# Statistics by tile, W1 in three loads, sixteen filler products and a new order in a fused attention and MLP kernel

## The chip, the cores and the metric

The kernel runs on one core of a Trainium2 chip. A core has five engines that run side by side: TensorE (PE, matrix products, with its weight loads shown as PEld), VectorE (DVE), ScalarE (ACT), GpSimd (POOL) and SyncE (SP, which here only issues DMA transfers). The metric is the device time of one execution in microseconds (us); lower is better.

## The reference

The input x has 2048 tokens of width 448. It is normalized, goes through a linear attention with 16 heads of 28 and through an MLP with 1792 hidden units, and both results are added to x:

```python
xn = _layernorm(x, axis=-1)
return x + _A_ref(xn, A_wqkv, A_w_phi, A_wo) + _B_ref(xn, B_w1, B_b1, B_w2)

def _A_ref(x, wqkv, w_phi, wo):
    ...
    pq = jnp.einsum("bhsd,hdf->bhsf", q, w_phi)
    pk = jnp.einsum("bhsd,hdf->bhsf", k, w_phi)
    phi_q = jnp.concatenate([_softmax(pq, axis=-1), _softmax(-pq, axis=-1)], axis=-1)
    phi_k = jnp.concatenate([_softmax(pk, axis=-1), _softmax(-pk, axis=-1)], axis=-1)
    kv = jnp.einsum("bhsf,bhsd->bhfd", phi_k, v)
    z  = jnp.einsum("bhsf->bhf", phi_k)
    num = jnp.einsum("bhqf,bhfd->bhqd", phi_q, kv)
    den = jnp.einsum("bhqf,bhf->bhq", phi_q, z)[..., None] + 1e-6
    ...

def _B_ref(x, w1, b1, w2):
    h = jnp.einsum("bsd,df->bsf", x, w1) + b1
    sp = jnp.log1p(jnp.exp(-jnp.abs(h))) + jnp.where(h > 0, h, jnp.zeros_like(h))
    act = h * jnp.tanh(sp)
    return jnp.einsum("bsf,fd->bsd", act, w2)
```

## The kernel before

The tokens are cut into 16 tiles t of 128; two tiles make a pair u (0 to 7). The kernel is a list of small steps, each named by a short word. The string ORDER is a list of these words, written out by hand or by a planner outside the kernel: the steps are called in that order, and each puts its instructions at the end of the queues of the engines that it uses. Each engine works through its own queue strictly in that order. What a step reads and writes is declared, and waits are derived from it; a wait holds up everything behind it on the same engine.

The steps, by their words:

- `lx0` to `lx6` load x (tiles 0-1, 2-3, 4-5, 6-7, 8-11, 12-15), `lkm`, `lvm`, `lkt` the weights of k and v (`lkt` their last 64 rows, in two transfers), `lp` w_phi, `lb` the bias b1, `l1m` and `l1t` W1 (rows 0 to 383 in one transfer, L271, and the last 64 rows twice, L276), `lo` and `l2` Wo and W2. A last letter s or a says whether SP or ScalarE issues it. `lqT0` to `lqT3` load Wq by a transposing DMA (L280); `qd` copies a part of it (L284).
- `st` makes the mean and variance of a tile or pair, on VectorE (two instructions, L456 and L458) or on ScalarE (L447 to L452), `rs` the reciprocal root (ScalarE L470 and L472, or POOL L464 and L467), `xn` the normalized pair (VectorE L491; with letter p on POOL, L486, after a small `shift` on VectorE). `xt` transposes it: letter m by a DMA from SP (L511), which also waits until tiles 0 and 15 of x have landed; else by TensorE (L499) with a copy out of PSUM (L504, L506).
- `z` is a run of filler products (L371) on TensorE; nothing reads their result. `wtk`, `wmk`, `wmq` fold w_phi into the weights of k and q (products L551 and L575), giving Wpk and Wpq; `b1` transposes the bias.
- `v`, `k`, `q` of a pair and `f0.c`, `f1.c` (the first MLP product for chunk c of the hidden units and half of the tokens) come in two parts: F, six products over 128 rows, and H, two products over 64 rows that run side by side in the two halves of the array (L426). The first part of the two takes a pair of PSUM banks; after the second the result is taken out: v by ScalarE or VectorE (L504, L506), k and q by two Exp (L613, L674) and f by one Mish (L693) on ScalarE. There are four pairs of banks; a new key takes the pair unused for longest, and waits for whoever empties it.
- `kn` normalizes half of a pair's k (VectorE L621 and L623, then POOL L625); `kv` sums k times v over all tokens (L642), one step per pair, and `kvz` masks the result and transposes it by DMA. `e` transposes a tile of q by DMA (L682). The q of three pairs shares three buffers, so a later Exp waits for an earlier `e`.
- `nd` forms numerator and denominator of a tile (L716, and eight VectorE instructions from L731 to L742), `ot` transposes the result by DMA (L750), `wo` (parts F and H, L832) and `g` (L816) make the output of a pair or tile, and `fin` adds x to it on VectorE (L781). `sto` and `stt` store a pair or tile; the last word of ORDER names the tile that is finished last, whose last 64 columns are done apart (L795 to L802) and whose store is split over ScalarE's and SP's queue (L843).

SP's queue holds nearly all loads, all transposes and all stores, in the order of ORDER. In the profile all of SP's transfers are on one queue (q1) and ScalarE's on another (q10).

## Time and profile before

| what | value |
|---|---|
| time, median of 3 runs | 153.97 us (153.91 to 154.64) |
| profiled execution: its span from first to last instruction | 152.5 us (its page gives no other time for it) |
| TensorE busy | 147.9 us, 97% |
| VectorE busy | 101.2 us, 66%; ScalarE 74.9 us, 49%; POOL 39.9 us, 26% |
| transfers | 39961 packets, 17.17 MB |
| engines in the first 50 us | VectorE and ScalarE are busy nine tenths and more in most slices |

The profile page names groups of instructions by line, engine and tiles ("out<-in"), gives their count, busy time and the mean length of one in ns, and the idle time of the engine before them with what ended it. The chain is followed back from the last instruction through whatever released each step. In the timeline each row has its start and length in us. TensorE's products overlap: one 379 ns long starts while the one before is still draining, so the distance of starts, not the length, is what a product costs.

### The profile page before, as it was taken

The numbers are of one execution on the slowest core, as the hardware profiler recorded it, in microseconds if no ns is written. First come the engines' busy times: TensorE is split into PE (matmuls) and PEld (weight loads), VectorE is DVE, ScalarE is ACT, GpSimd is POOL, SyncE is SP. The second block draws the span as 40 slices with busy tenths as digits, with TensorE's granted clock in tenths as the row PEclk, the third lists the DMA queues.
The fourth block names the chain that finished last, engine by engine and source line by source line (L and its number), as shares of the span: only waits on it lengthen the run. The fifth ranks groups of instructions, "written<-read, shape, count | busy, mean of one in ns | idle before, by whom it ended". The sixth has DMA issues, their size and how long they took to land.

```text
span 152.5 us, 2888 instructions
## 1 busy us (share of the span) xinstructions
PE 147.9 (97%) x1181; PEld 72.7 (48%) x1181; DVE 101.2 (66%) x227; ACT 74.9 (49%) x91; POOL 39.9 (26%) x58
## 2 busy tenths in 40 slices
PE   7899999999998999999999999999999999999993
PEld 2365444454443466444444444555555555455552
DVE  1699997999999203198999847798695970311221
ACT  4888899898599996757459657100000000000000
POOL 7452552499999950000000000000000000000000
PEclk9999999999999999999999999999999999999999
DMA  5995576889969176830379941030206111110302
GB/s 130 274 238 97 175 136 127 177 236 257 189 141 192 24 160 55 135 71 0 64 149 302 338 75 25 4 62 6 54 0 195 50 34 26 60 34 0 120 0 90
DMA packets 39961, 17.17 MB, mean 113 GB/s; under 512 B 33932, under 2 KB 39180, under 8 KB 39948
## 3 DMA queue, kind: packets, MB, share of 16 engines
q1 hardware_dynamic: 39804, 16.89, 49.2%
q8 instruction: 9, 0.15, 0.4%
q10 hardware_dynamic: 144, 0.10, 0.2%
q14 instruction: 4, 0.03, 0.1%
HBM read 7.02 MB, written 1.84 MB: 58 GB/s over the span
## 4 chain that ended last, share of the span: by engine, by line
PE 82%; DMA 7%; ACT 6%; SPq 2%; DVE 0%; issue 0%; ACTq 0%
PE PS L426 40%; PE PS L816 28%; PE PS L832 7%; DMA EqT<-actT 4%; DMA Wkv<-in_A_wqkv_dram 3%; PE PS L716 3%; PE PS L642 2%; ACT actT L613 2%; ACT actT L693 1%; ACT actT L674 1%; PE PS L575 1%; ACT L693 1%; ACT v_all L504 1%; SPq L268 1%; SPq L682 1%; PE PS L551 0%
## 5 line engine op out<-in xcount | busy, mean ns | idle before, releaser
L426 PE MATMUL PS<-xnT,W 128*128 128x512 bf16 (+1 forms) x224 | 46.3, 379 | 0.0
L816 PE MATMUL PS<-W,actT 128*128 128x448 bf16 (+1 forms) x224 | 42.8, 351 | 0.0
L693 ACT ACTIVATE actT<-PS,b1T 128x1024 bf16<-128x1024 f32 x28 | 30.3, 1114 | 13.1 <-PE PS L426 13.0
L816 PEld LDWEIGHTS PS<-W,actT 128*128 128x128 bf16 x224 | 21.8, 98 | 20.2 <-issue 0.4
L426 PEld LDWEIGHTS PS<-xnT,W 128*128 128x128 bf16 (+1 forms) x224 | 17.6, 97 | 23.7 <-issue 5.1
L625 POOL TENSOR_TENSOR actT<-actT,rSk 128x896 bf16<-128x896 bf16 x16 | 26.6, 1701 | 4.4 <-DVE rSk L623 4.4
L781 DVE TENSOR_TENSOR x_all<-PS,x_all 128x448 bf16<-128x448 f32 (+1 forms) x16 | 9.6, 617 | 20.9 <-PE PS L816 17.7
L621 DVE TENSOR_REDUCE Sk<-actT 128x32 f32<-128x896 bf16 x16 | 16.7, 1042 | 0.9 <-ACT actT L613 0.9
L613 ACT ACTIVATE actT<-PS 128x896 bf16<-128x896 f32 x16 | 13.7, 940 | 0.4 <-PE PS L426 0.4
L426 PE MATMUL PS<-Wpq,xnT 128*128 128x448 bf16 (+1 forms) x64 | 12.9, 353 | 0.5 <-ACT actT L693 0.5
L426 PE MATMUL PS<-Wpk,xnT 128*128 128x448 bf16 (+1 forms) x64 | 12.7, 353 | 0.0
L426 PE MATMUL PS<-Wkv,xnT 128*128 128x448 bf16 (+1 forms) x64 | 12.6, 353 | 0.0
L731 DVE COPY Sq<-PS 128x16 f32<-128x16 f32 x32 | 4.0, 167 | 10.8 <-PE PS L716 10.8
L456 DVE BATCH_NORM_STATS2 stats<-x_all 128x6 f32<-128x448 bf16 x14 | 8.5, 605 | 3.4 <-DMA x_all<-in_A_x_dram 3.4
L739 DVE TENSOR_TENSOR v_all<-v_all 128x464 f32<-128x464 f32 x16 | 10.3, 642 | 0.6
L735 DVE TENSOR_TENSOR v_all<-PS,Sq 128x464 f32<-128x464 f32 x16 | 10.3, 641 | 0.5
L742 DVE TENSOR_TENSOR xn<-v_all,rden 128x448 bf16<-128x448 f32 x16 | 10.0, 625 | 0.6
L737 DVE TENSOR_TENSOR v_all<-PS,Sq 128x464 f32<-128x464 f32 x16 | 10.1, 629 | 0.0
L674 ACT ACTIVATE actT<-PS 128x896 bf16<-128x896 f32 x10 | 8.5, 932 | 1.7 <-DMA EqT<-actT 1.7
L426 PEld LDWEIGHTS PS<-Wpq,xnT 128*128 128x128 bf16 (+1 forms) x64 | 5.3, 97 | 6.5 <-issue 1.1
L426 PEld LDWEIGHTS PS<-Wpk,xnT 128*128 128x128 bf16 (+1 forms) x64 | 5.3, 97 | 6.1 <-issue 1.9
L426 PEld LDWEIGHTS PS<-Wkv,xnT 128*128 128x128 bf16 (+1 forms) x64 | 5.0, 97 | 5.7 <-issue 1.5
(86 smaller groups left out, 118.0 us busy)
## 6 DMA issues: line engine op xcount, KB each, us to landing
W<-in_B_w_dram SPq DMA_DIRECT2D x1, 1568.0 KB, 7.8
out_dram<-x_all SPq DMA_DIRECT2D x7, 224.0 KB, 2.2
W<-in_B_w_dram SPq DMA_DIRECT2D x1, 1344.0 KB, 9.0
x_all<-in_A_x_dram SPq DMA_DIRECT2D x4, 224.0 KB, 3.2
x_all<-in_A_x_dram SPq DMA_DIRECT2D x2, 448.0 KB, 4.6
Wkv<-in_A_wqkv_dram SPq DMA_DIRECT2D x2, 336.0 KB, 4.5
Wo<-in_A_wo_dram SPq DMA_DIRECT2D x2, 336.0 KB, 3.9
W<-in_B_w_dram SPq DMA_DIRECT2D x2, 224.0 KB, 3.6
```

The costliest lines, as they stand in the source:

```text
L426: ins = e.matmul(o, lhs(c, k), rhs(c, k), start=first and c in (0, 3), stop=not first and c in (2, 3))
L613: op("ACT", lambda e, s=s: e.activation(E_of(u)[:, s, :, :], two(b, D), ACT.Exp, scale=1.0 if s == 0 else -1.0), r=[pb(b), pb(b + 1)], w=[ ...
L621: op("DVE", lambda e: e.tensor_reduce(Sk[u][:, s, :], Eh(), AX.X, ALU.add), r=[("E", u, s)], w=[("Sk", u, s)], tag=f"Sk{u}.{s}")
L625: op("POOL", lambda e: e.tensor_tensor(Eh(), Eh(), ap_on(rSk[u][:, s, 0:1], [[1, 2 * H], [0, DH]]), ALU.mult), r=[("E", u, s), ("rSk", u, ...
L674: op("ACT", lambda e, s=s: e.activation(Eq_of(u)[:, :, s, :].rearrange("p i (h n) -> p i h n", n=64)[:, :, :, 0:QP], two(b, D).rearrange(" ...
L693: op("ACT", lambda e: e.activation(actT[:, fc, q * 1024:(q + 1) * 1024], bank(b, 2), ACT.Mish, bias=b1T[:, fc:fc + 1]), r=[("b1T",), pb(b) ...
L735: op("DVE", lambda e: e.tensor_tensor(tv(t1[i]), num(0), sx(1), ALU.mult), r=[pb(b), pb(b + 1), ("Sq", i, 1)], w=[("t1", i)], tag=f"ta{t}")
L737: op("DVE", lambda e: e.tensor_tensor(tv(t2), num(1), sx(0), ALU.mult), r=[pb(b), pb(b + 1), ("Sq", i, 0)], w=[("t2",)], tag=f"tb{t}")
L739: op("DVE", lambda e: e.tensor_tensor(t1[i], t1[i], t2, ALU.add), r=[("t1", i), ("t2",)], w=[("t1", i)], tag=f"tc{t}")
L742: op("DVE", lambda e: e.tensor_tensor(o_sb[(t // 2) % 2][:, t % 2, :].rearrange("p (h d) -> p h d", d=DH), t1[i][:, :, 0:DH], ap_on(rden[i ...
L816: ins = e.matmul(bank(b)[:, 0:width(t)], actT[:, fc, tok(t)], W2[:, fc, 0:width(t)], start=first and fc == 0, stop=last and fc == FC - 1)
L832: ins = e.matmul(bank(b)[:, 0:n], oT_of(u)[lo:hi, cc * P:(cc + 1) * P], Wo[lo:hi, cc, 0:n], start=first and c in (0, 3), stop=last and c i ...
```

## The change

The products stay the same but for four more fillers. What changes is:

- `st` and the statistics go by tile: `st6d` is tile 6 on VectorE, `st2a` tile 2 on ScalarE (before, a pair at a time, with letter b one tile on each). `rs` gets a letter t: logarithm and root for each of the two tiles by itself on ScalarE. A tile's xn waits for its own root only.
- rows 0 to 383 of W1 come in three transfers, `l1m0` to `l1m2`, each a word of its own.
- the fillers read a constant 1.0 that the framework writes at the start; the tile of zeros and its memset are gone, and there are 16 instead of 12 (`z16`).
- which step first waits for the old contents of an ot buffer follows the order (`homes_taken`) instead of being the even pair.
- ORDER is new throughout. Pairs 3 and 1 are transposed on TensorE instead of 2 and 3; pairs 6 and 7 are normalized on POOL instead of 5; ScalarE makes the statistics of tiles 2 and 5 instead of 5 and 7; w_phi is loaded by ScalarE's queue; b1 is loaded and transposed much later; Wo and W2 are loaded earlier.

```diff
@@ -145,18 +145,19 @@
 
 
 ORDER = """
-table lx2s zero lx3s pv st2b pw lkms lps pi pm st3b rs3a lkts z12 pp lbs rs2p lx1s xn2d xn3d wtk0b xt2b wtk1b lvms
-lx4s lqT2 st1 bd pk lqT0 xt3a b1 wmk0b lqT1 rs1a wmk1a xn1d st5 rs5p v2Fd lqT3 v3Fa v3Ha k2H v2Ha k3H qd xt1m lx0s
-st4 k2F rs4p wmq0d xn4d xn5p wmq1a k3F v1Fd st0 q3F k1H q3H lx6s st6 v1Hd q2H q2F rs6p st7 k1F q1F rs0p xt4m xt5m
-xn6d k4F rs7p k4H e6 v5Hd xn0d xt6m xn7d kn4.1 q1H k5H xt0m v5Fd k5F kn5.0 v6Fd kn5.1 k6F k0H xt7m ep e7 v6Ha k7H
-l1ts l1ms k6H k7F kn6.0 k0F kn6.1 e3 q6F e2 v0Fa kn2.1 kn7.1 v4Fd v0Ha v4Hd kn4.0 q6H v7Hd kn3.0 v7Fa q4F e4 e12
-f1.2H q4H e9 f0.2H kn2.0 e13 f0.2F kn7.0 f0.0F f1.2F f0.1F f0.0H f0.1H f1.3H q5H kn1.0 f1.3F kn0.1 e8 q0F q0H f0.3H
-kn0.0 q7H kn3.1 e5 e1 q5F q7F f0.3F f1.7F kv7 kn1.1 kv0 kv4 kv6 kv3 kv2 kv1 e0 kv5 e10 f1.1H kvz f1.7H f1.8H f1.1F
-f1.8F f0.6F e14 e11 f1.5H f0.6H nd2 f0.10F f1.5F nd1 f0.10H f0.5H f0.5F f1.11F nd3 ot1m f1.11H nd0 f0.13H f0.13F e15
-f1.12F f1.0F f1.0H ot0m f1.12H los wob nd6 f1.13F f0.7F f1.10H f0.7H nd7 l2s ot3m f1.13H f1.10F f0.4F f0.4H nd5
-f0.12H f0.9H f0.9F f0.12F nd4 f0.11H f0.8H f0.8F f0.11F f1.4F f1.6H f1.4H nd10 ot2m f1.9H f1.9F f1.6F wo3F wo3H nd11
-nd13 nd12 ot5m ot6m g7 g6 g10 g11 wo5H nd15 nd14 wo2H wo5F ot7m g5 sto3 g4 wo2F wo6F sto5 wo6H wo1H nd9 nd8 wo1F sto2
-g12 g2 g14 g13 wo7F wo0F ot4m wo0H sto6 wo4H wo7H g3 g0 wo4F g1 g8 stt14 sto0 g9 sto1 sto4 g15 stt15
+lpa lx1s pi lx3s lkms lkts lvms table lx2s st3d pp pw pm lqT1 st6d st2a pv st7d z16 rs3t rs1a xn3d xn1d lqT2 lqT3 lqT0
+wtk0b bd xt3b wtk1b xt1d wmk0b st4d v3Fd wmk1d st5a lx6s qd rs2t xn2d lx0s v1Fd v1Ha v3Ha st15d st14d rs7p k1F wmq1d
+st12d xn7p wmq0a lx4s st10d xt2m k3F st9d st8d rs4p st11d rs5p st13d k1H l1ts k3H xn4d xt7m q3H q1H q1F l1m2s rs6p q3F
+xn5d xn6p q2F k2F kn3.0 xt4m v2Fd v2Hd xt5m q2H st0d st1d k2H xt6m v7Ha v7Fa rs0p k7F k4F k7H l1m1s e3 xn0d k4H xt0m
+v5Hd k6H lbs pk kn1.1 kn3.1 k6F v5Fd kn7.0 kn6.1 k5F k0F k5H e6 kn5.0 v6Ha q4H kn2.0 e2 k0H q4F l1m0s e7 v6Fd ep q6F
+v0Fd b1 v0Hd q6H f1.3H f0.0H f1.3F e8 f1.1F f0.0F kn5.1 kn7.1 kn0.1 v4Fa e9 v4Ha kn1.0 f1.0H e13 e12 f1.1H f0.1H kn4.1
+kn4.0 f1.0F f0.1F f1.2F los q7H kn6.0 q5H kn0.0 f1.2H q0H e5 e4 kn2.1 q7F q5F q0F f1.13F kv5 kv0 kv7 kv4 kv3 kv6 kv1
+kv2 f0.13H f1.13H f0.12H f0.12F f0.13F e0 kvz wob f0.3F e1 f1.8H f0.3H f0.11H l2s nd0 f1.8F f0.11F f1.10F nd1 f1.10H
+ot0m e10 e14 e11 f1.9H nd2 f1.9F f1.12F f0.8F f1.12H f0.7H f0.8H nd3 f0.7F f0.2F f1.7F nd5 e15 f1.7H f1.11H f0.2H
+f1.11F f0.9F nd4 f1.4H f0.10H f0.9H f1.4F f0.10F ot1m ot2m f0.6F f0.4H f0.5H f0.6H nd12 f0.5F f0.4F f1.5F nd13 f1.6H
+ot6m nd8 f1.5H f1.6F g0 g1 wo6F nd7 wo0H nd9 wo6H g12 g13 ot4m wo2F wo0F g5 wo2H nd6 ot3m nd10 nd11 g4 g8 g7 g9 wo3H
+ot5m nd15 nd14 wo4H ot7m g6 wo4F g14 g2 g3 g11 wo1F wo7F wo5F wo1H wo5H wo7H sto1 wo3F g10 sto6 sto0 sto5 sto3 sto4
+g15 stt14 sto2 stt15
 """
...
-    zeros = sb("zeros", [P, 2], BF16)
     junk = [sb(f"junk{i}", [P, D], BF16) for i in range(2)]
...
+    def load_chunk(eng, name, dst, src, c):
+        dma(eng, lambda e: e.dma_start(dst[:, c, :], src[c * P:(c + 1) * P, :]), w=[(name, 0, c)], tag=f"ld{name}.{c}")
+
...
     def rows_of(name):
-        return [(name, 0), ("Wt", 0), ("Wt", 1)] if name in ("Wk", "Wv") else [(name, i) for i in range(3)]
+        if name in ("Wk", "Wv"):
+            return [(name, 0), ("Wt", 0), ("Wt", 1)]
+        return [("W1", 0, c) for c in range(3)] + [("W1", 1), ("W1", 2)]
...
     def warm(n):
         b = take1()
+        one = nc.const_aps.tensor(1.0, (P, 1), BF16)
 
         def f(e):
             for _ in range(n):
-                ins = e.matmul(bank(b)[:, :], ap_on(zeros[:, 0:1], [[0, P]]), ap_on(zeros[:, 0:1], [[0, TCW]]), start=True,
-                               stop=True)
+                ins = e.matmul(bank(b)[:, :], ap_on(one, [[0, P]]), ap_on(one, [[0, TCW]]), start=True, stop=True)
             return ins
-        pe(f, [("zeros",)], [pb(b)], f"warm{n}")
+        pe(f, [], [pb(b)], f"warm{n}")
...
-    def ln_stats(u, both=False):
-        for t in (2 * u, 2 * u + 1):
-            if both and t % 2:
-                i = u % 2
-                op("ACT", lambda e, t=t: e.activation(junk[i][:], x_all[:, t, :], ACT.Copy, scale=1.0 / D,
-                                                      accum_out=mv[:, t, 0:1]),
-                   r=[("x", t), ("junk", i)], w=[("mean", t), ("junk", i)], tag=f"sm{t}")
-                op("ACT", lambda e, t=t: e.mul(rmean[:, i:i + 1], mv[:, t, 0:1], D ** -0.5), r=[("mean", t)],
-                   w=[("rmean", i)], tag=f"rm{t}")
-                op("ACT", lambda e, t=t: e.activation(junk[i][:], x_all[:, t, :], ACT.Square, bias=rmean[:, i:i + 1],
-                                                      scale=-D ** -0.5, accum_out=mv[:, t, 1:2]),
-                   r=[("x", t), ("rmean", i), ("junk", i)], w=[("mv", t), ("junk", i)], tag=f"sq{t}")
-                continue
-            op("DVE", lambda e, t=t: e.bn_stats(stats[:, t, :], x_all[:, t, :]), r=[("x", t)], w=[("st", t)],
-               tag=f"bn{t}")
-            op("DVE", lambda e, t=t: e.bn_aggr(mv[:, t, :], stats[:, t, :]), r=[("st", t)], w=[("mv", t), ("mean", t)],
-               tag=f"ag{t}")
+    def ln_stats(t, eng):
+        if eng == "ACT":
+            i = t // 2 % 2
+            op("ACT", lambda e: e.activation(junk[i][:], x_all[:, t, :], ACT.Copy, scale=1.0 / D, accum_out=mv[:, t, 0:1]),
+               r=[("x", t), ("junk", i)], w=[("mean", t), ("junk", i)], tag=f"sm{t}")
+            op("ACT", lambda e: e.mul(rmean[:, i:i + 1], mv[:, t, 0:1], D ** -0.5), r=[("mean", t)], w=[("rmean", i)],
+               tag=f"rm{t}")
+            op("ACT", lambda e: e.activation(junk[i][:], x_all[:, t, :], ACT.Square, bias=rmean[:, i:i + 1],
+                                             scale=-D ** -0.5, accum_out=mv[:, t, 1:2]),
+               r=[("x", t), ("rmean", i), ("junk", i)], w=[("mv", t), ("junk", i)], tag=f"sq{t}")
+            return
+        op("DVE", lambda e: e.bn_stats(stats[:, t, :], x_all[:, t, :]), r=[("x", t)], w=[("st", t)], tag=f"bn{t}")
+        op("DVE", lambda e: e.bn_aggr(mv[:, t, :], stats[:, t, :]), r=[("st", t)], w=[("mv", t), ("mean", t)], tag=f"ag{t}")
...
-               r=[("mv", a), ("mv", a + 1)], w=[("lnv", u)], tag=f"vare{u}")
+               r=[("mv", a), ("mv", a + 1)], w=[("lnv", a), ("lnv", a + 1)], tag=f"vare{u}")
             op("POOL", lambda e: e.tensor_tensor(rstd[:, a:b], lnv[:, a:b], mhalf[:], ALU.pow),
-               r=[("lnv", u), ("eps",)], w=[("rstd", u)], tag=f"rstd{u}")
+               r=[("lnv", a), ("lnv", a + 1), ("eps",)], w=[("rstd", a), ("rstd", a + 1)], tag=f"rstd{u}")
             return
-        op("ACT", lambda e: e.activation(lnv[:, a:b], mv[:, a:b, 1], ACT.Ln, bias=eps_col[:]),
-           r=[("eps",), ("table",), ("mv", a), ("mv", a + 1)], w=[("lnv", u)], tag=f"ln{u}")
-        op("ACT", lambda e: e.activation(rstd[:, a:b], lnv[:, a:b], ACT.Exp, scale=-0.5),
-           r=[("lnv", u)], w=[("rstd", u)], tag=f"rstd{u}")
+        for n, m in ((a, b),) if eng == "ACT" else ((a, a + 1), (a + 1, b)):
+            op("ACT", lambda e, n=n, m=m: e.activation(lnv[:, n:m], mv[:, n:m, 1], ACT.Ln, bias=eps_col[:]),
+               r=[("eps",), ("table",)] + [("mv", t) for t in range(n, m)], w=[("lnv", t) for t in range(n, m)], tag=f"ln{n}")
+            op("ACT", lambda e, n=n, m=m: e.activation(rstd[:, n:m], lnv[:, n:m], ACT.Exp, scale=-0.5),
+               r=[("lnv", t) for t in range(n, m)], w=[("rstd", t) for t in range(n, m)], tag=f"rstd{n}")
...
-        home = [("oT", u)] + ([x for n in oT_home[u // 2][2] for x in home_rows[n]] if u % 2 == 0 else [])
+        home = [("oT", u)] + ([x for n in oT_home[u // 2][2] for x in home_rows[n]] if u // 2 not in homes_taken else [])
+        homes_taken.add(u // 2)
...
-        add(f"st{u}", ln_stats, u)
-        add(f"st{u}b", ln_stats, u, True)
+        for t in (2 * u, 2 * u + 1):
+            for eng, c in (("DVE", "d"), ("ACT", "a")):
+                add(f"st{t}{c}", ln_stats, t, eng)
         add(f"xt{u}b", xT, u, "both")
-        for eng, c in (("ACT", "a"), ("POOL", "p")):
+        for eng, c in (("ACT", "a"), ("POOL", "p"), ("tiles", "t")):
             add(f"rs{u}{c}", ln_rstd, u, eng)
...
-        add(f"l1m{c}", load_main, eng, "W1", W1, B_w1)
+        for i in range(3):
+            add(f"l1m{i}{c}", load_chunk, eng, "W1", W1, B_w1, i)
...
-    for n in (1, 2, 4, 8, 12):
+    for n in (4, 8, 10, 12, 14, 16, 18, 20):
         add(f"z{n}", warm, n)
```

More of the change, by code (lines that the diff above doesn't have):

```diff
@@ L239, in _kernel @@
                  "Wp1": [("Wp", 1, h, c) for h in range(2) for c in range(2)]}
+    homes_taken = set()
     def oT_of(u):
@@ L309, in table @@
            tag="table")
-    def p_zero():
-        op("POOL", lambda e: e.memset(zeros[:], 0.0), w=[("zeros",)], tag="zeros")
     def p_ident():
@@ L480, in ln_pair @@
                                                        ALU.mult),
-               r=[("mean", a), ("mean", a + 1), ("rstd", u)], w=[("sh", u)], tag=f"sh{u}")
+               r=[("mean", a), ("mean", a + 1), ("rstd", a), ("rstd", a + 1)], w=[("sh", u)], tag=f"sh{u}")
         for t in (a, a + 1):
@@ L488, in ln_pair @@
                         op0=ALU.mult, op1=ALU.add),
[L489 removed]
+                       r=[("x", t), ("sh", u), ("rstd", t)], w=[("xn", u % NXN, t % 2, n)], tag=f"xn{t}.{n}")
                 else:
```

5 lines of the change are left out of this document (2 added, 3 removed).

## The prediction

> **What bounds the kernel now.** I read the busy shares first, then the chain that ended last, then the timeline of single engines where the chain leaves TensorE.
>
> ```profile
> span 152.5 us, 2888 instructions
> PE 147.9 (97%) x1181; PEld 72.7 (48%) x1181; DVE 101.2 (66%) x227; ACT 74.9 (49%) x91; POOL 39.9 (26%) x58
> ...
> 7.97 0.65 PE PS L551 x8
> ...
> 15.19 15.00 PE PS L426 x86
> ...
> 35.20 6.42 DMA EqT<-actT
> ...
> 46.90 8.57 PE PS L426 x44
> 55.47 3.27 PE PS L642 x128
> ...
> 119.29 10.59 PE PS L816 x56
> ...
> 149.53 0.56 DVE x_all L781
> ```
>
> TensorE is the bound: from 7.97 to 149.5 the chain is nearly all PE. 56 products of 448 columns take 10.59 us, 0.189 each, so the last two thirds have no room. A new order can gain only in four places: the start (before 7.97), the places where PE waits, the cost of changing from one kind of product to the other, and the end (after 149.5). Where the chain leaves PE (31 to 47 us) PE waits twice:
>
> ```profile
> 38.27 1.30 PE L426 MATMUL PS<-Wpq,xnT 128*128 128x448 bf16 x6
> 39.60 0.39 PE L426 MATMUL PS<-xnT,W 64*128 64x512 bf16 x2
> ...
> 46.90 0.36 PE L426 MATMUL PS<-Wpq,xnT 64*128 64x448 bf16 x2 [0.46 <-ACT actT L693]
> ...
> 30.47 0.59 SPq L271 DMA_DIRECT2D W<-in_B_w_dram  x1
> 31.10 9.71 SPq L682 DMA_TRANSPOSE EqT<-actT  x3
> ...
> W<-in_B_w_dram SPq DMA_DIRECT2D x1, 1344.0 KB, 9.0
> EqT<-actT SPq DMA_TRANSPOSE x10, 3.3
> ...
> 41.69 1.73 ACT L674 ACTIVATE actT<-PS 128x896 bf16<-128x896 f32 x2 [1.67 <-DMA EqT<-actT]
> ```
>
> W1 in one load, issued at 30.47, lands 9.0 us later, at 39.5: the first product on it starts at 39.60, about 0.1 late (the sixth at 0.189 from 38.27 starts at 39.22, plus 0.285 as below). The three transposes queued behind that load take 9.71 us to issue; one lands at 41.6 (35.20 + 6.42), ScalarE waits 1.67 us for its buffer, and PE pays 0.46 at 46.90, with the product's tail (379 ns long, issued every 216) 0.6.
>
> **The start.** Loads lead to the first weight transposes.
>
> ```profile
> 0.95 5.30 PE L371 MATMUL PS<-zeros 128*128 128x512 bf16 x12 [0.95 <-POOL zeros L314]
> 2.71 1.20 SPq L276 DMA_DIRECT2D Wkv<-in_A_wqkv_dram  x2
> 6.02 5.11 SPq L280 DMA_TRANSPOSE WqT<-in_A_wqkv_dram  x4
> ...
> 6.70 0.63 PE L551 MATMUL PS<-ident,Wkv 128*112 128x128 bf16 x8 [0.45 <-DMA Wkv<-in_A_wqkv_dram]
> 7.97 0.65 PE L551 MATMUL PS<-ident,Wkv 128*112 128x128 bf16 x8 [0.23 <-DMA Wkv<-in_A_wqkv_dram]
> ...
> 13.70 1.07 SPq L268 DMA_DIRECT2D x_all<-in_A_x_dram  x2
> ...
> x_all<-in_A_x_dram SPq DMA_DIRECT2D x2, 448.0 KB, 4.6
> ```
>
> Twelve fillers take 5.30 us, 0.44 each, and end at 6.25; at the pace of the later products a 512-wide one takes 0.216 (0.189 x 512 / 448). Sixteen, from about 0.85 (no memset of zeros), end at 7.9 if all are slow and at 6.2 if half are; I take 7.2. wtk0 and xt3 then end near 8.05, and wtk1, which waits for the tails of Wkv (7.97 here; the same bytes stand before them, only the phi load of 24.5 KB changes queue), starts 0.1 later: **+0.1** (bounds -0.2, +0.6). Removing the memset, the per-tile statistics and rstd (0.5 us more on ScalarE for each of two pairs) and the earlier Wv are hidden by that wait; without it the rstd pieces would cost their 0.5. The phi load moves to ScalarE's queue, where that engine has only a table to load. The b1 load and its transpose move behind xt0m and v0F: the first Mish, near 41, is their reader, and b1's two changes of rows cost what the place saves, within 0.05. Which pairs PE transposes (3 and 1 for 2 and 3) changes no count on PE or SP, and homes_taken only follows the order.
>
> The fillers' 0.44 is twice that 0.216, and they stay slow to their end. The Trainium skill ("TensorE: Matmul & The Clock Gate", Part 1, on the clock gate) says that TensorE runs at half rate until about 3.4 us of sustained work, counted in a window that runs free of the kernel. By that rule the slow stretch can end anywhere from some 4.4 to 7.8 us, another point in each execution; the trace agrees with the half rate, and one trace can't show the free window. It would make rival C an accident of single runs, not a cost of the change.
>
> **Kinds of product.** Parts F use 128 rows, parts H and nd half of them. A change between them costs PE time:
>
> ```profile
> 106.65 0.73 PE L816 MATMUL PS<-W,actT 128*128 128x448 bf16 x3
> 107.31 0.36 PE L832 MATMUL PS<-Wo,WqT 64*128 64x448 bf16 x2
> ...
> 107.95 0.35 PE L832 MATMUL PS<-Wo,Wkv 64*128 64x448 bf16 x2
> 108.24 0.55 PE L832 MATMUL PS<-Wo,WqT 128*128 128x448 bf16 x2
> ```
>
> The third full product starts at 107.03 (106.65 + 2 x 0.189) and the half one at 107.31: 0.28 instead of 0.189, and back 107.95 to 108.24 likewise. So 0.095 per change. Counting neighbours in the two ORDER strings (g, kv, F against H, nd; b1 apart): 42 changes before, 39 after: **-0.3**, certain. The work itself is the same 170 steps.
>
> **W1 in three loads, transposes apart.** Two more issues (0.59 each) on SP. Chunks 2 and 1 go out near 21 and 26 us, chunk 0 after e2 near 33.4 (my sum of SP's issues, 1.3 each transpose, with xt0m waiting for xn0); a load of 448 KB takes 4.6 by the x row, so W1 is whole at 38.0, and f1.3H, the first to want it, is due at 38.8. xt0, e3 and e2 queue behind 448 KB instead of 1344. Both waits above go: **-0.7** (bounds -0.1, if e7 behind chunk 0 keeps the larger one, and -0.7). What comes next: exq6 needs e7, but also q6H, at 38.7, so the cover is PE itself.
>
> **The new order of VectorE, POOL and SP.** VectorE is nearly full until 50 us, and the new order loads it more: one more v evacuation, Wpk's second half and xnT1, less one xn pair that goes to POOL.
>
> ```profile
> 15.47 1.14 DVE L506 CAST Wpq<-PS 128x448 bf16<-128x448 f32 x2
> 17.76 1.74 POOL L486 TENSOR_SCALAR xn<-x_all,rstd,shift 128x448 bf16<-128x448 bf16 x3 [1.11 <-DVE shift L479]
> 19.82 0.59 DVE L456 BATCH_NORM_STATS2 stats<-x_all 128x6 f32<-128x448 bf16 x1
> ...
> 20.55 1.06 DVE L506 CAST v_all<-PS 128x896 bf16<-128x896 f32 x1
> ...
> 23.00 2.46 DVE L491 TENSOR_SCALAR xn<-x_all,mv,rstd 128x448 bf16<-128x448 bf16 x9
> 30.32 24.89 POOL L625 TENSOR_TENSOR actT<-actT,rSk 128x896 bf16<-128x896 bf16 x15 [0.74 <-DVE rSk L623]
> 33.36 1.03 DVE L621 TENSOR_REDUCE Sk<-actT 128x32 f32<-128x896 bf16 x1
> ...
> 34.70 1.03 DVE L621 TENSOR_REDUCE Sk<-actT 128x32 f32<-128x896 bf16 x1
> ```
>
> Statistics of a tile take 0.73 (19.82 to 20.55), an xn pair 0.82 (2.46 / 3), a k_norm half 1.34 (33.36 to 34.70), POOL's share of it 1.66 (24.89 / 15). SP reaches the WqT transposes at 4.4 instead of 6.02 (phi, b1 and x4 no longer stand before them), ends them near 9.5, and issues x6, x0, x4 behind. VectorE has done xn2 at about 13.5 (the last WqT transpose lands some 4 us after its issue at 8.2, then the copy qd and xn2's 0.82) and then stands at the statistics of tile 15. If x6 has landed by then, its queue to the end of ve2 is 8 x 0.73 + 1.14 + 2 x 0.82 + 0.2 + 1.34 + 1.05 = 11.2: 24.7 to 24.9. PE gets to k7F, which takes v2's pair of banks, after 10 parts F (1.13 each), 10 parts H (0.19), three Wp products (0.4) and 6 changes from 9.4 (where v3F can start, wmk1 now coming after it): 24.4. So PE waits there **0.4** (bounds 0, if the sums are out by half a us, and 1.5, if x6 takes 4.6 us or more from its issue at 9.5: 14.1, which holds up q3H as well, behind Wpq's evacuation). I take 0.4 because fewer bytes are queued before x6 than before x4 here. POOL: xn7 and xn6 (1.74 each), rs0 and the second mask come in front of or between the k_norms; the last one ends near 56.3, and kv2 wants it near 58, so 1.5 us of cover; beyond it each us costs one. By the same sums xnT7, xnT4, xnT6 and xnT0 land 0.2 to 1.1 us before PE asks. Wo and W2 go out earlier, ahead of the ot transposes; what stands behind W2 is read 30 us later, and that covers its landing.
>
> **The end.** Stores are queued as sto1, 6, 0, 5, 3, 4, 14, 2, 15.
>
> ```profile
> 142.62 5.63 SPq L846 DMA_DIRECT2D out_dram<-x_all  x3
> 147.26 0.62 DVE L781 TENSOR_TENSOR x_all<-PS,x_all 128x448 bf16<-128x448 f32 x1 [2.02 <-PE PS L816]
> ...
> 150.31 0.33 SPq L843 DMA_DIRECT2D out_dram<-x_all  x1
> ...
> 143.50:144.50 1.00, 1.00 (x7) 0.54 (x6) 0.00 (x0) 0.00 (x0) 0.00 (x0) 1.00 1.03 378
> ```
>
> Now one store (224 KB) goes out after the add at 147.26. After the change sto5 needs g10, the last but one, and sto3, sto4, stt14, sto2 stand behind it: 1008 KB between 147.9 and 150. At 378 GB/s and a full DMA that is 2.7 us, from 148.5 to 151.2 or so, and the last 16 KB stand behind them: **+0.3** (bounds 0 and 0.8).
>
> **The sum.** 0.1 - 0.3 - 0.7 + 0.4 + 0.3 = -0.2. The profiled span is 152.5 and the median 153.97, so 1.5 lie around it; the page gives that execution no time of its own, and I carry the 1.5 over. Forecast: 153.8.
>
> **Rivals.** (A) Every just-in-time arrival holds and the stores drain in time: none of the 0.1, the 0.4 and the 0.3 appears, 153.0, and with the start's -0.2 152.8. For it: each new wait is inside my half us of error; against it: three of them must hold together. (B) Slower: tile 15's statistics stand at the head of VectorE's queue before x6 lands. From 13.5 each us of delay shifts Wpq's evacuation, ve2, xn0 and all k_norms by one; at 15, 1.5 us more, 155.3. Slower by 0.5% from 14.5 on. Against it: x6 goes out 4.8 us sooner than now (9.5 for 14.3). (C) All sixteen fillers run slow to 7.9 and hold up wtk0 and with it wtk1, by 0.6: 154.4. (D) The split does not do what it says: three loads of 4.6 us are 13.8 against 9.0 in one, so W1 gets slower in sum, and chunk 0, the last, stands behind e2. From 5.4 us to landing on, PE waits at f1.3H one for one; at 6.2 that is 0.8, and 154.6. Against it: chunks 2 and 1 have long landed then. The Trainium skill ("DMA: Bandwidth & Descriptors", Bandwidth) advises loads of 1 MiB or more for three quarters of the peak rate; the trace agrees in direction (448 KB in 4.6 us, 1344 KB in 9.0), so by that rule alone the split is a loss and the time is D's.
>
> **How the numbers follow.** Forecast 0.33, A 0.30, B 0.17, C 0.08, D 0.12. A measurement of this kernel tells about 0.5%: under 153.2 is faster, over 154.74 slower. Faster: most of A (0.27) and the lower side of the forecast (0.09), 0.36; slower: B and the upper end of D, 0.22; within: 0.42. The range takes in A, with 0.4 for my error in its terms, 152.4, and B, 155.3; the forecast's own is 153.1 to 154.5.
>
> **What would show it.** After: W1's loads land before 38 and no wait for EqT on ScalarE near 41 (split right); PE waits for VectorE's v_all near 24 (the 0.4), for Wpq's evacuation near 16 (B), or nowhere (A); wtk1 starts near 8.05 (start); the last store lands more than 2.5 us after PE's end (tail). I am wrong if PE has a wait over 1 us before 60 us, or if kv waits on POOL.

## The result, and the profile after

The changed kernel takes 155.91 us (median of 4 runs, 155.80 to 156.28). Against the kernel before, measured beside it, the ratio is 1.012, with a 95% interval of 1.009 to 1.014: slower, where 153.8 us and no change were forecast, and 0.6 us outside the range. The profiled execution took 155.94 us with a span of 154.2 us; before, the span was 152.5, so 1.7 us are to be found. Medians and ratios leave out an execution that lies over 1.5% above the fastest of its kernel.

These lines are from the page of the changed kernel: span, busy shares and W1's loads.

```profile
span 154.2 us, 2908 instructions
...
PE 148.2 (96%) x1185; PEld 73.1 (47%) x1185; DVE 103.4 (67%) x228; ACT 74.2 (48%) x94; POOL 40.9 (27%) x58
...
W<-in_B_w_dram SPq DMA_DIRECT2D x3, 448.0 KB, 4.1
```

PE's busy time hardly moved (147.9 to 148.2), so the 1.7 us are waits. The chain that ended last, which before was PE's from 7.97 on but for the stretch from 30 to 47 us, now runs mostly through VectorE, with some of POOL, from 13.79 until 40.69:

```profile
9.74 4.02 DMA x_all<-in_A_x_dram
...
15.36 1.04 DVE Wpq L507 x2
...
24.22 1.03 DVE v_all L507
...
38.89 0.12 DVE epsT L367
39.02 1.46 issue
40.47 0.17 DVE b1T L507
...
40.69 16.15 PE PS L430 x84
```

It starts at x6's load (9.74), passes the second statistics, Wpq's evacuation, v2's evacuation, and ends at b1T. PE's timeline has a wait at each of these places (in brackets; the tail of the product in front, about 0.17 us, comes on top):

```profile
16.46 4.06 PE L430 MATMUL PS<-Wpq,xnT 64*128 64x448 bf16 x22 [0.54 <-DVE Wpq L507]
...
25.31 2.93 PE L430 MATMUL PS<-Wpk,xnT 128*128 128x448 bf16 x16 [0.41 <-DVE v_all L507]
...
39.28 0.38 PE L430 MATMUL PS<-xnT,W 64*128 64x512 bf16 x2
40.69 4.38 PE L430 MATMUL PS<-xnT,W 64*128 64x512 bf16 x20 [1.03 <-DVE b1T L507]
...
56.77 3.33 PE L643 MATMUL PS<-actT,v_all 128*60 128x112 bf16 x128
```

Counted from one product's start to the next, less the pace of an undisturbed product, these waits are 0.70 us (q3H at 16.46), 0.58 (k7F at 25.31) and 1.19 (f0.0H at 40.69); two small ones add 0.17. Before, there were 0.1 and 0.6 (W1 and EqT) and two small ones of 0.15. So kv starts at 56.77 instead of 55.40, 1.37 later: the start gains 0.25 (the second half of the key-weight transposes at 7.72 instead of 7.97), the waits cost 1.8 more, and the rest (kinds of product, order) gains 0.15. Behind kv, PE gains 0.2 more: its end is at 151.18 (150.61 + 0.57 below) against 150.02, 1.16 later. The end takes 0.54 longer: 3.03 us from PE's end to the span's end, before 2.48. The 1.37, the -0.21 and the 0.54 make the 1.7.

The timeline of the changed kernel: VectorE's wait for x6, VectorE and POOL around the largest wait, and the end on PE and SP:

```profile
13.79 0.63 DVE L458 BATCH_NORM_STATS2 stats<-x_all 128x6 f32<-128x448 bf16 x1 [1.00 <-DMA x_all<-in_A_x_dram]
...
37.70 1.03 DVE L507 CAST v_all<-PS 128x896 bf16<-128x896 f32 x1
38.65 0.21 DVE L364 TENSOR_REDUCE epsT<-ident 128x1 f32<-128x4 bf16 x2
38.89 1.66 DVE L367 SCALAR_TENSOR_TENSOR epsT<-epsT 128x1 f32<-128x1 f32 x1
40.47 0.16 DVE L507 CAST b1T<-PS 128x14 f32<-128x14 bf16 x1
...
38.84 1.70 POOL L626 TENSOR_TENSOR actT<-actT,rSk 128x896 bf16<-128x896 bf16 x1
...
150.61 0.57 PE L800 MATMUL PS<-W,actT 128*128 128x64 bf16 x14
...
149.07 2.30 SPq L848 DMA_DIRECT2D out_dram<-x_all  x5
151.47 0.39 SPq L845 DMA_DIRECT2D out_dram<-x_all  x1
```

An instruction on one element per partition (ep's last, L367) takes 1.66 us. It starts just after a product of POOL has started (38.84) and ends just after that product's end: 40.550 against 40.537. Behind it on VectorE stands b1T's evacuation (40.47). And PE waits for that: b1's transpose was put into a bank that f0.0H takes, two allocations later. The prediction did not mention ep, and priced b1's new place at nothing.

### The profile page after: what moved, and what is told of

Same layout as the page of the kernel before. It is cut to its first block, busy times and chain, and to the rows that moved or that the text cites. A ratio compares the mean times of both kernels' runs of the same rounds, so it can differ in the third digit from the quotient of the medians.

```text
span 154.2 us, 2908 instructions
## 1 busy us (share of the span) xinstructions
PE 148.2 (96%) x1185; PEld 73.1 (47%) x1185; DVE 103.4 (67%) x228; ACT 74.2 (48%) x94; POOL 40.9 (27%) x58
## 4 chain that ended last, share of the span: by engine, by line
PE 71%; DVE 14%; SPq 5%; DMA 3%; POOL 3%; issue 2%; DVEq 0%; POOLq 0%
PE PS L430 32%; PE PS L818 27%; PE PS L834 7%; DVE Sk L622 4%; SPq L285 3%; DVE stats L458 3%; PE PS L717 3%; DMA x_all<-in_A_x_dram 3%; PE PS L643 2%; POOL rstd L467 2%; DVE v_all L507 2%; DVE rSk L624 1%; DVE mv L459 1%; SPq L270 1%; SPq L281 1%
## 5 line engine op out<-in xcount | busy, mean ns | idle before, releaser
L430 PE MATMUL PS<-xnT,W 128*128 128x512 bf16 (+1 forms) x224 | 45.8, 379 | 1.0 <-DVE b1T L507 1.0
L694 ACT ACTIVATE actT<-PS,b1T 128x1024 bf16<-128x1024 f32 x28 | 30.8, 1114 | 13.6 <-PE PS L430 13.2
L732 DVE COPY Sq<-PS 128x16 f32<-128x16 f32 x32 | 4.0, 168 | 13.8 <-PE PS L717 13.8
L430 PE MATMUL PS<-Wkv,xnT 128*128 128x448 bf16 (+1 forms) x64 | 12.8, 353 | 0.0
L430 PE MATMUL PS<-Wpq,xnT 128*128 128x448 bf16 (+1 forms) x64 | 12.1, 353 | 0.5 <-DVE Wpq L507 0.5
```

The source lines that it names most:

```text
L430: ins = e.matmul(o, lhs(c, k), rhs(c, k), start=first and c in (0, 3), stop=not first and c in (2, 3))
L694: op("ACT", lambda e: e.activation(actT[:, fc, q * 1024:(q + 1) * 1024], bank(b, 2), ACT.Mish, bias=b1T[:, fc:fc + 1]), r=[("b1T",), pb(b) ...
```

## Experiments

The question was which of these waits carry the loss, and why an instruction of one element takes 1.66 us. Theory P: an instruction of VectorE that reads two tensors from SBUF (the on-chip memory) cannot run while POOL is inside its product. Rival F: VectorE ran out of code, since a load of instructions falls at 39.8 us among transposing DMAs (the trace does not say for which engine). All kernels are the changed one with the shown edit, unless the text says otherwise. The kernel before was timed again beside them: its medians were 154.4 to 154.8 us over 17 to 24 runs, where the 153.97 above rests on three. Against these the changed kernel's 155.91 us would be 1.007 to 1.010 rather than 1.012, still slower. It was not timed again itself, so a gain over it is read in us, from its 155.91 and from the profiles; the ratios say where a run stands to the kernel before.

### ep moved to where POOL is idle

```diff
-... xn2d lx0s ... v6Fd ep q6F ...
+... xn2d ep lx0s ... v6Fd q6F ...
```

> The step ep (two reductions and one SCALAR_TENSOR_TENSOR of one element, on VectorE) moves from 38.65 to just behind xn2d, near 12.8, where VectorE is idle and POOL does nothing; all other queues stay. In the changed kernel the SCALAR_TENSOR_TENSOR took 1.66 us and ended 13 ns after POOL's TENSOR_TENSOR (40.537 and 40.550). Theory P (an instruction of VectorE with two inputs in SBUF waits for the instruction that POOL is in): it takes 0.1 to 0.2 us, b1T's evacuation starts near 39.0, PE's wait of 1.03 there goes, kv starts near 55.7 and the time falls by 1.0 to 1.2, to about 154.8. Rival F (VectorE's instruction fetch at 39.8 meets the transposing DMAs): the instruction count before that point is the same, so a gap of about 1.5 us stays near 39 to 40 on VectorE, and the time stays at 155.9.

Measured: 154.82 us, ratio 1.001 (0.999 to 1.004). ep's last instruction takes 0.16 us, b1T is evacuated as soon as PE has made it, and PE's timeline has no wait there. On VectorE:

```profile
13.15 0.16 DVE L367 SCALAR_TENSOR_TENSOR epsT<-epsT 128x1 f32<-128x1 f32 x1
...
39.08 0.17 DVE L507 CAST b1T<-PS 128x14 f32<-128x14 bf16 x1 [0.25 <-PE PS L688]
```

kv starts at 55.58, 1.19 earlier, as much as the wait was worth; the other differences of this execution (a start 0.2 later, 0.4 less at q3H, 0.3 more at k7F) nearly cancel. No gap stays near 40, though as many instructions stand in front of that point as before and a load of instructions still falls there, at 40.3: F fails.

### The same place, with one tensor input

```diff
-scalar_tensor_tensor(epsT[:, 2:3], epsT[:, 0:1], DEN_EPS / 2, epsT[:, 1:2], ALU.mult, ALU.add)
+tensor_scalar(epsT[:, 2:3], epsT[:, 0:1], DEN_EPS / 2, epsT[:, 1:2], op0=ALU.mult, op1=ALU.add)
```

> Nothing moves; the one SCALAR_TENSOR_TENSOR of ep, whose two inputs are tensors in SBUF, is written as a TENSOR_SCALAR with one tensor input and the other value as the scalar of its partition. Theory P: 0.1 to 0.2 us instead of 1.66 although POOL is in the same TENSOR_TENSOR, PE's wait for b1T goes, 1.0 to 1.2 us faster than the changed kernel, near 154.8. Rival F (fetch), and a third, R (the wait is for the two reductions in front of it): the 1.66 stays, 155.9.

Measured: 154.77 us, ratio 0.999 (0.996 to 1.002). The rows of VectorE and of POOL:

```profile
38.56 0.21 DVE L367 TENSOR_SCALAR epsT<-epsT 128x1 f32<-128x1 f32 x1
...
38.50 1.70 POOL L626 TENSOR_TENSOR actT<-actT,rSk 128x896 bf16<-128x896 bf16 x1
```

Same place, same sums, POOL in the same kind of product from 38.50 to 40.20: 0.21 us. So neither the two reductions in front nor the place is the cause, but the second tensor input while POOL is in its product. In each of the ten profiled kernels that keep the two-input form in the stretch of POOL's products (the kernel before among them), it ended 12 to 16 ns after POOL's product, whether it took 0.35, 1.01 or 1.66 us:

```text
kernel           starts   took    end behind POOL's product
before           31.68    0.348   0.016
changed          38.89    1.657   0.013
W1 together      42.23    1.011   0.014
b1 early         38.60    1.659   0.014
```

Before, the instruction came 0.35 us before POOL's end by chance. The Trainium skill ("SBUF — State Buffer", SBUF: two separate sides) states this rule: VectorE and GpSimd share one pair of ports as an exclusive lock, held for a whole instruction, and an operation of VectorE with two SBUF inputs (against a GpSimd operation that reads SBUF), or in a mode that uses two ports, needs it. The traces here agree, with the 12 to 16 ns as their number.

### b1 early, ep in place

The load of b1 goes to ScalarE's queue at the start, its transpose behind xt1.

```diff
-lpa lx1s ... wtk1b xt1d wmk0b ... k6H lbs pk ... v0Fd b1 v0Hd ...
+lpa lba lx1s ... wtk1b xt1d b1 wmk0b ... k6H pk ... v0Fd v0Hd ...
```

> ep stays where it is; the load of b1 goes to ScalarE's queue at the start and its transpose on PE stands behind xt1d, so that no bank waits for b1T's evacuation near 40. Theory: the SCALAR_TENSOR_TENSOR still takes up to 1.66 us, but PE does not wait for it; the next reader of VectorE's work there is f1.1F (v0's pair of banks), due near 41.45 against the end of that evacuation near 41.5, so 0.1 is left of the 1.19 and the time falls by about 1.1, of which the two changes of rows around b1 are 0.1: 154.8. If the pair for f1.1F is what counts, the fall is under 0.5.

Measured: 155.31 us, ratio 1.005 (1.003 to 1.006): part of the gain. ep's instruction takes 1.66 us as before (38.60, in the table above), and PE's next wait is this:

```profile
41.32 2.76 PE L430 MATMUL PS<-xnT,W 128*128 128x512 bf16 x12 [0.48 <-DVE v_all L507]
```

The wait no longer goes through b1's bank but through v0's pair of banks, whose evacuation stands behind ep too. I had put 0.1 there and it is 0.64, counted from start to start like the 1.19 (0.48 in the row). kv starts at 55.78, 0.99 earlier; the rest of that is smaller waits at q3H and k7F in this execution. So VectorE's stop is the cause and b1's bank was only the first to pass it on.

### Wpq's evacuation ahead of the statistics

```diff
-v3Ha st15d st14d rs7p k1F wmq1d
+v3Ha k1F wmq1d st15d st14d rs7p
```

> On VectorE the evacuation of Wpq's first half stands ahead of the statistics of tiles 15 and 14, which wait for x6 until 13.79. Theory B of the prediction (tile 15's statistics at the head of the queue): Wpq is cast from 14.2 on, as its product ends, q3H starts when PE gets there (near 15.8), and PE's stall of 0.7 at 15.57 goes. But the statistics then end 0.2 to 1.0 later, and ve2 (24.22) with them, where PE's stall of 0.58 begins: what is gained at 16 is given back at 25 if ve2 stays at 24.2. Theory: time between 155.2 (all kept) and 155.9 (all given back); by the order on VectorE, which fills the idle 1.00 us partly with the cast (1.12), ve2 can come 0 to 0.3 earlier, so I expect the stall to move: 155.7.

Measured: 156.73 us, ratio 1.014 (1.012 to 1.016): worse than the theory allowed. The wait at 16 goes, and comes back larger:

```profile
14.15 1.16 DVE L507 CAST Wpq<-PS 128x448 bf16<-128x448 f32 x2 [1.16 <-PE PS L576]
...
17.93 0.16 DVE L480 SCALAR_TENSOR_TENSOR shift<-mv,rstd 128x2 f32<-128x2 f32 x1 [0.42 <-POOL rstd L467]
...
25.13 1.03 DVE L507 CAST v_all<-PS 128x896 bf16<-128x896 f32 x1
...
26.21 2.93 PE L430 MATMUL PS<-Wpk,xnT 128*128 128x448 bf16 x16 [1.59 <-DVE v_all L507]
```

The hole in VectorE's queue is not filled but stretched to 1.16 us, since the cast waits for its product; the statistics then come later, POOL's rstd with them, and VectorE has a second hole of 0.42. v2's evacuation comes 0.9 later (25.13 for 24.22). What counts here is how long VectorE needs up to v2, its holes included; this swap made the holes longer.

### x6's load earlier

```diff
-table lx2s ... lqT1 ... wmk1d st5a lx6s qd
+table lx2s lx6s ... lqT1 ... wmk1d st5a qd
```

> The load of tiles 12 to 15 (x6) goes ahead of the four transposes of WqT on SP, 4.6 instead of 9.74. Theory B of the prediction (tile 15's statistics stand at the head of VectorE's queue and wait for x6): x6 lands near 9.5, the hole of 1.00 us at 12.8 goes and everything on VectorE behind it comes 1.0 earlier; the stall at 15.57 (0.70) goes, the one before k7F (0.58) shrinks to 0.2 to 0.3, the one for b1T stays about as it is since both engines move: 154.8 to 155.0. Against it: the four transposes are issued 0.5 later and run beside 448 KB; if the copy qd (11.77) gets later by more than 1 us, the product wmq1 (13.34) and with it everything is late, and the time is 155.9 or more.

Measured: 155.37 us, ratio 1.005 (1.002 to 1.008), less of a gain than the 154.8 to 155.0 expected. In the profile kv starts at 55.79, 0.98 earlier; the waits for Wpq and for v2 are gone altogether, and the one for b1T is all that PE's timeline names up to kv:

```profile
23.25 1.03 DVE L507 CAST v_all<-PS 128x896 bf16<-128x896 f32 x1
...
39.72 4.38 PE L430 MATMUL PS<-xnT,W 64*128 64x512 bf16 x20 [0.98 <-DVE b1T L507]
...
55.79 3.34 PE L643 MATMUL PS<-actT,v_all 128*60 128x112 bf16 x128
```

v2's evacuation starts at 23.25 instead of 24.22. The first two waits of the changed kernel thus have one cause: VectorE stands still from 12.8 to 13.8, waiting for x6.

### v2's evacuation earlier on VectorE

```diff
-xn6p q2F k2F kn3.0 xt4m v2Fd v2Hd xt5m q2H st0d st1d k2H ... v7Fa rs0p k7F
+xn6p q2F k2F xt4m st0d v2Fd v2Hd st1d xt5m q2H k2H ... v7Fa rs0p kn3.0 k7F
```

> On VectorE tile 0's statistics go ahead of v2's evacuation (ve2), tile 1's behind it, and the first half of k_norm 3 behind both; on POOL rstd of pair 0 goes ahead of that k_norm. PE's, ScalarE's and SP's orders stay. Theory (what PE waits for near 25 and 40 is the length of VectorE's queue, with two holes in it): ve2 runs as soon as v2H ends, 23.85 instead of 24.22, so the stall of 0.58 before k7F shrinks to 0.15 to 0.2; rstd of pair 0 is done near 26.6, so the hole of 1.14 before xn0 (27.86) goes and VectorE stands 0.8 to 0.9 further from there on. The stall for b1T depends on where POOL's instruction then ends: between 0 and 1.2. Together 0.4 to 1.6 less, 154.3 to 155.5, I expect 155.0. Rival: the stall before k7F stays because k_norm 3 was not what held ve2: 155.9 or, if only the hole goes, 155.0.

Measured: 156.08 us, ratio 1.009 (1.006 to 1.012): nothing gained, where 155.0 was expected. The wait before k7F is gone (v2's evacuation at 23.21), and so is the hole before xn0, but in its place stands a piece of xn0 that takes 1.77 us; the rows are VectorE's, POOL's and PE's:

```profile
26.30 2.19 DVE L492 TENSOR_SCALAR xn<-x_all,mv,rstd 128x448 bf16<-128x448 bf16 x3
...
26.46 1.70 POOL L626 TENSOR_TENSOR actT<-actT,rSk 128x896 bf16<-128x896 bf16 x1 [0.34 <-DVE rSk L624]
...
31.98 1.59 PE L430 MATMUL PS<-Wpk,xnT 128*128 128x448 bf16 x8 [0.47 <-DMA xnT<-xn]
...
40.42 4.38 PE L430 MATMUL PS<-xnT,W 64*128 64x512 bf16 x20 [0.83 <-DVE b1T L507]
```

The three pieces otherwise take 0.9 together. POOL's product of k_norm 3, which I had moved to this place, ends at 28.162, and xn0's piece of 64 columns, begun at 26.513, ends at 28.281 (a short MEMSET of POOL, from 28.101 to 28.247, stands in between). The piece has one tensor input. By the Trainium skill ("VectorE: DVE Perf Modes", Mode 2×_2P) such an instruction on tensors in SBUF can read one tensor through both ports; this row agrees with a lock that holds it up too. So the next late thing was xn0's transpose, and the b1T wait stayed.

### The order of the stores

```diff
-sto5 sto3 sto4 g15 stt14 sto2 stt15
+sto3 sto4 g15 stt14 sto2 sto5 stt15
```

> Only SP's order at the end: the store of pair 5, which waits for the add that ends at 149.04, goes behind the stores of pairs 3, 4, tile 14 and pair 2, whose data lie ready at 147.44. Theory (the last 0.53 us are bytes queued in front of the last store): the DMA engines, idle between 147.3 and 149.2, take 784 KB of that in time, the last store lands 1.7 to 1.9 us after its issue instead of 2.27, as in the kernel before (1.72), and the time falls by 0.4 to 0.5, to 155.5. Rival (the tail is the fixed time of a store): 155.9.

Measured: 155.15 us, ratio 1.001 (0.998 to 1.004), a larger gain than the 155.5 expected. From the issue of the last store on SP to the end of the span it is 2.2 us (151.20 to 153.4), before the change 2.2 (150.31 to 152.5), in the changed kernel 2.7 (151.47 to 154.2). That is the 0.5 of the theory: bytes in front of the last store. The time fell by 0.25 us more than that, and so much lies in front of kv in the profile: it starts at 56.50, 0.27 earlier, in a stretch that this edit does not touch. In this execution PE's first product of v starts 0.9 later, q3H does not wait, k7F waits 0.15 and f0.0H 0.9. I take the 0.27 for scatter, which no run shows by itself, and only the 0.5 for the stores.

### W1's three loads together

```diff
-... l1m2s ... l1m1s e3 ... l1m0s e7 ...
+... l1m2s l1m1s l1m0s e3 ... e7 ...
```

> The three loads of W1 stand together where the second stood (26.06), ahead of the transposes e3, xt0, e2 and e7; the split stays, the spreading goes. Theory (the 0.7 came from the transposes not standing behind a whole W1): 1344 KB in one go take 9 us, W1 is whole near 36.5 and no product waits for it, but the transposes behind it land up to 6 us later: PE waits for xnT0 (k0, due near 33) or for ScalarE, which waits for EqT, by 0.6 to 3 us; 156.5 to 158.9. Rival (the loads are hidden anyway, the position is worth nothing): 155.9.

Measured: 159.30 us, ratio 1.028 (1.022 to 1.033), more than the 158.9 that the theory allowed. The rows are SP's, with xt0's issue behind the loads, PE's wait for it, and a line of the view by stretches (busy time of PE, of its weight loads, of VectorE, ScalarE and POOL, then the granted clock, here 0.50, the DMA share and GB/s):

```profile
25.55 1.54 SPq L277 DMA_DIRECT2D W<-in_B_w_dram  x3
...
28.58 3.72 SPq L512 DMA_TRANSPOSE xnT<-xn  x1
...
34.45 2.88 PE L430 MATMUL PS<-Wpk,xnT 128*128 128x448 bf16 x8 [2.83 <-DMA xnT<-xn]
...
34.49:37.91 3.42, 3.42 (x14) 1.10 (x14) 0.12 (x1) 0.54 (x1) 2.22 (x2) 0.50 1.22 106
```

xt0, which takes 1.22 us to issue in the changed kernel, takes 3.72 behind 1344 KB, and PE stands idle for 2.83. That is not all that it loses: right behind the wait, from 34.49 to 37.91, the granted clock is a half, and products of 448 columns start 0.37 us apart instead of 0.19, which costs 1.6 more. All four runs show it in their mean clock, 0.989 instead of 1.00. Against this, f0.0H and q3H no longer wait, and kv starts 2.83 later in sum. So the position of the loads is worth much: what stands between them keeps the transposes in time. The experiment does not price the split itself.

### The split alone, in the kernel before

Tails and chunk 2 of W1 behind x6's load, chunk 1 behind e6, chunk 0 where the whole load was.

```diff
-lx6s st6 ... k4H e6 v5Hd ... v6Ha k7H l1ts l1ms k6H ...
+lx6s l1ts l1m2s st6 ... k4H e6 l1m1s v5Hd ... v6Ha k7H l1m0s k6H ...
```

> The kernel before with W1's load alone changed: tails and chunk 2 behind x6's load (14.8), chunk 1 behind e6 (22.7), chunk 0 where the whole stood (30.5). Theory (the split's term of the sum is right alone): the waits at 39.6 (0.1) and 46.9 (0.6) go, 0.7 less than the kernel before, provided that the transposes xt6, xt0 and xt7 behind chunk 1 come no more than 0.6 us later; 153.3 with the kernel before at 154.0. Rival: the transposes behind the chunks arrive late, PE waits for xnT near 30, and the time is the same or up to 2 us more.

Measured: 155.28 us (median of five), ratio 1.005 (1.001 to 1.008). The rival was right:

```profile
23.66 0.58 SPq L275 DMA_DIRECT2D W<-in_B_w_dram  x1
24.47 4.68 SPq L516 DMA_TRANSPOSE xnT<-xn  x3
...
31.18 4.84 SPq L687 DMA_TRANSPOSE EqT<-actT  x3
...
23.79 1.59 PE L431 MATMUL PS<-Wpk,xnT 128*128 128x448 bf16 x8 [0.32 <-DVE mv L463]
...
29.68 1.30 PE L431 MATMUL PS<-Wkv,xnT 128*128 128x448 bf16 x6 [1.36 <-ACT actT L618]
...
57.09 3.34 PE L647 MATMUL PS<-actT,v_all 128*60 128x112 bf16 x128
```

Both old waits are gone (the three transposes take 4.84 us to issue, where they took 9.71), worth 0.7. But PE waits at 23.79 and 29.68, with the tails 0.5 and 1.5, since the x transposes behind the chunks come later: the one issued at 19.68 lands at 23.65, 4.0 us later (before 3.0), and xt6, issued at 24.47, lands at 29.55, 5.1 us later (before 3.0). The rows name VectorE and ScalarE, but the pair of banks that v6 takes had been emptied by 27.21, and PE starts 0.135 us after each of these landings, just as it does where a row names such a transpose (with W1 together it lands at 34.32 and PE starts at 34.45). kv starts 1.69 later: 0.42 in the start of this execution, 2.0 in new waits, -0.7.

### Twelve fillers

```diff
-st7d z16 rs3t
+st7d z12 rs3t
```

> The changed kernel with twelve fillers instead of sixteen. Theory (the second half of the key-weight transposes waits for the tails of Wkv, near 7.1 to 7.7, whatever stands before it): no change, 155.9 within 0.3. Rival (the four fillers bring the full clock earlier, which is why the start gained 0.4 instead of losing 0.1): the early products run at the lower clock for longer, the first product of v starts 0.3 to 0.6 later, 156.3.

Measured: 156.07 us, ratio 1.010 (1.007 to 1.012): no change that can be told. The key-weight transposes start 0.28 later than in the changed kernel (8.00), and kv at 56.79, only 0.02 later: VectorE's wait for x6 takes up what PE gains at the start. Over the eleven profiles with the changed kernel's sixteen fillers that place lies between 7.62 and 8.53, in the two with the order of before at 7.97 and 8.34, so one trace can't price it to 0.25. The fillers start 0.43 us apart at first and 0.22 later; in the eleven profiles the pace changes at 3.75 in one and at 6.78 in another, with all others between. So one trace can't tell what four fillers do to the clock either.

### Three moves together, and a fourth

First ep, x6 and the stores, each as above.

> The changed kernel with three moves together: ep behind xn2d, the load x6 ahead of the transposes of WqT, and pair 5's store behind the others. Theory (the loss is these waits, each at its own place): against the changed kernel -1.1 to -1.2 (b1T), -0.7 to -1.0 (q3H and part of k7F), -0.5 (stores), together -2.3 to -2.7, 153.2 to 153.6, which is faster than the kernel before by 0.2 to 0.5% or level with it. What may take it back: with PE earlier by 2 us at 55 us, POOL's last k_norm (58.04 in the changed kernel, some 2.5 earlier here, since VectorE feeds it earlier) could reach kv; then a wait for POOL's actT shows in front of kv and the time is up to 154.5.

Measured: 154.03 us, ratio 0.996 (0.995 to 0.998): 1.9 us less than the changed kernel, where 2.3 to 2.7 were expected. PE's timeline has one wait left up to kv:

```profile
24.98 2.93 PE L430 MATMUL PS<-Wpk,xnT 128*128 128x448 bf16 x16 [0.69 <-DVE v_all L507]
...
55.16 3.34 PE L643 MATMUL PS<-actT,v_all 128*60 128x112 bf16 x128
```

With x6 early, VectorE has no hole at 13 any more, so ep's instructions, which take 0.41 us there, lengthen the queue up to v2's evacuation. That starts 0.58 later than with x6 alone (23.83 for 23.25); at the statistics right behind ep it is 0.22, and for the rest I have no cause. The fourth takes ep to VectorE's idle time before the first x lands, and v2's evacuation forward, now with POOL's second mask in front of k_norm 3:

```diff
-pi lx3s ... kn3.0 xt4m v2Fd v2Hd xt5m q2H st0d st1d ... v7Fa rs0p k7F ... pk kn1.1
+pi ep lx3s ... xt4m st0d v2Fd v2Hd st1d xt5m q2H ... v7Fa rs0p pk kn3.0 k7F ... kn1.1
```

> The kernel of the three moves, with ep at the very start of VectorE's queue and with v2's evacuation brought forward: tile 0's statistics ahead of it, tile 1's behind it, k_norm 3 behind both, and on POOL the second mask between rstd of pair 0 and k_norm 3's product. Theory P (an operation of VectorE that uses both of its read ports waits for POOL's instruction): in the run with the reordered VectorE queue one piece of xn0 took 1.77 us because POOL's product of k_norm 3 ran from 26.46 to 28.16; with the mask in between (2 us of short instructions) xn0 is done by 27.2, no piece takes over 0.5, and the stall of 0.69 before k7F is 0 to 0.15: 153.3 to 153.5, 0.6 to 0.8% faster than the kernel before. Rival (PE's gain there meets the next late thing, the transpose xt0 that waits for SP behind e3): 153.8 to 154.0, no faster than the three moves.

Measured: 153.70 us, ratio 0.994 (0.992 to 0.996), the lowest median here, between the 153.3 to 153.5 of the theory and the 153.8 to 154.0 of the rival. Both hold in part:

```profile
26.16 0.85 DVE L492 TENSOR_SCALAR xn<-x_all,mv,rstd 128x448 bf16<-128x448 bf16 x3
...
25.70 1.78 PE L430 MATMUL PS<-Wpk,xnT 128*128 128x448 bf16 x10 [0.20 <-DMA xnT<-xn]
...
31.69 1.59 PE L430 MATMUL PS<-Wpk,xnT 128*128 128x448 bf16 x8 [0.32 <-DMA xnT<-xn]
```

xn0's pieces are back at 0.85 together and k7F waits no more; PE now waits for two transposes instead, 0.8 in sum from start to start, and kv starts at 55.21, no earlier than with three moves (55.16). The two intervals overlap, so a gain of the fourth move over the three isn't shown.

## Why the prediction was wrong

**The step that failed** is the sentence on b1: that its load and transpose move behind xt0m and v0F, and that its two changes of rows cost what the place saves, within 0.05. It cost 1.19, of the 1.9 by which the sum (-0.2, measured 1.7) was out; VectorE's term was 0.9 too small and the end's 0.2, and the start came out 0.35 better. I asked when b1T's reader comes and not which bank the transpose takes, who takes that bank next (f0.0H, two allocations later) and what stands in front of the evacuation on VectorE: ep, moved from 31.5 to 38.7. ep was in the profile with 0.35 us for one element (L363), a number that should have been asked about, as POOL was in its product then. In the new place ep's last instruction was held for 1.66 us until POOL's product ended, b1T's evacuation stood behind it, and f0.0H waited for the bank. Moving ep alone brought the 1.2 back.

**VectorE, +0.4**, was right in mechanism and too small. k7F did wait for v2's evacuation, 0.58 for the 0.4, near the predicted 24. But rival B's threshold was wrong: I let x6 cost from 13.5 on, summed up to v2's evacuation only. It landed at 13.77, and with the two statistics (1.5 us) and the two casts behind it Wpq's half was ready at 16.4, which PE wanted at 15.76. So q3H waited 0.70, and by the same rows any landing after about 13.1 would have cost. The bounds (0 to 1.5) held the sum, 1.28. With x6 loaded early kv came 0.98 sooner.

**The end, +0.3**, measured 0.54, inside its bounds, and by the mechanism told: with pair 5's store last, the span's end follows the last issue by 2.2 us again.

**The start, +0.1**, came out at -0.25 in this execution. It is not a cost, but as wide as its scatter, and it did not count, since x6 took up what was gained.

**W1 in three loads, -0.7**, fits: the three chunks, issued apart, take 4.1 us each (median), more in sum than the 9.0 of one load, as D had it, but hidden; W1 is read without a wait, and no EqT wait is left at 41. No run prices the split in the new order by itself. With the loads together another and larger wait comes, for a transpose. What I had not said is how much hangs on the place of each chunk: in the kernel before, the same split in other places cost 2.0 of waits.

**Kinds of product, -0.3**, came out at -0.2: behind kv two changes fewer stand (24 for 26), and PE gains 0.2 there. In front of kv there are 16 in both kernels, so the count of 39 should have been 40; the 0.15 that PE gains there beside its waits is not of this kind and stays open.

**The rivals.** Against A: of the three costs that it struck out, the start's did not appear, but VectorE's and the end's did, each larger than forecast. C did not appear: here the fast pace began at 5.04, and the last filler started at 6.14. In four other profiles (ep early, one tensor input, x6 early, three moves) the key-weight transposes stand right behind the last filler, but their second half starts at 7.78 to 8.07, within the range of the others. D's chunk 0 was in time: it landed at 37.79, and f1.3H read it at 39.28. The signs named in advance, a wait for v_all near 24, one for Wpq's evacuation near 16 and a late last store, all appeared, and so did the one that would make me wrong, a wait over 1 us before 60 us.

## What to carry to other kernels

When a small step moves, ask three things of its new place: which bank it borrows and who takes that next, what stands in front of its evacuation, and whether an instruction in that queue needs something that another engine holds. The full queue here was not helped by swapping two of its members; it was helped by closing a hole in it, as the early load did, and each hole closed made the next arrival the late one. A tiny instruction with a long row is worth a question even while it costs nothing.
